# Weight tiles of four feed-forward matrices begun at other byte offsets

## The chip, the cores and the metric

The kernel runs on one NeuronCore of one Trainium2 chip. The time is device microseconds from launch to end; before the change it is 2638.81 us, the median of three runs (2638.7 to 2639.36).

## The reference

Three stages follow each other on 24,576 rows of 128 numbers in float32 (two batches of 12,288):

```
kv_pool = kv averaged over 4x4 patches          # 2 x 768 keys x 128
k = v   = kv_pool @ w_sr
a       = softmax(q @ k.T / sqrt(128))          # rows x 768
x       = a @ v
h = x @ w_in1 ; x = (h * clip(h + 3, 0, 6) / 6) @ w_out1   # 128 -> 2048 -> 128
h = x @ w_in2 ; out = (h * cos(h)) @ w_out2                # 128 -> 2048 -> 128
```

## The kernel before

The rows go through in 48 blocks of 512, with features on the partitions and the block's 512 rows along the free dimension. A number that TensorE is to multiply precisely is held as a sum of two float32r parts, hi and lo, and one product is made of three matmuls: hi by hi, lo by hi and hi by lo. Each of the four weight matrices (in1, out1, in2, out2) lies in SBUF for the whole program as a hi and a lo array of 16 slices of 128x128; a slice is 512 bytes in each partition.

A unit (`plan_unit`) is one layer, one block and two of the 16 slices. `ff_in` (L845) issues six matmuls of 512 columns (L849, L850, L851 for each slice): the slice of `w_in` is the stationary operand, loaded by a weight load that the profile shows as PEld, and the block's `x` tile is the moving one. ScalarE, VectorE and GpSimd make the gated value and split it into a `hi` and a `lo` tile. `ff_out` (L853) then issues six matmuls (L857, L858, L859) with the slice of `w_out` stationary and `hi` or `lo` moving. With 48 blocks, two layers and eight units there are 768 units, and so 768 x 12 = 9,216 such matmuls, 2,304 on each weight matrix.

Attention adds, for each block, 24 float32r matmuls of 384 columns for the scores (L651; a q tile is stationary, the keys move) and six float32 products for the values (L773; `v_all` is stationary, the transposed softmax tile moves), each of which the trace shows as two records. Three early blocks are transposed by TensorE (L565, L742), the others by DMA.

The order on each engine is worked out before the program is written: `Plan.run` simulates the engines with fixed costs and due times and writes the instructions in that order.

All SBUF tiles come from one pool that lays them one behind another in the order in which they are made: constants, keys, values, the eight weight arrays (L283 to L287), then the `w`, `hi`, `lo` and `x` tiles of 4,096 bytes. In the built program the address of each of these, from `w_sr_sb` to the last `x`, leaves 192 when divided by 512; `ident` alone leaves 128. The weights are written once, in the first part of the program, in 16 pieces of four slices, the hi part by ScalarE (L399), the lo part by GpSimd or VectorE (L407).

Of the kernel before, what the change touches and what calls it, by code (L numbers as in the profile page):

```python
# [11 lines left out]
F32R = mybir.dt.float32r  # L12
# [24 lines left out]
SPARE = 5  # L37

NSCR = 3

BY_PE = 3

# [200 lines left out]
def attention_ffn_ffn_kernel(  # L243
# [13 lines left out]
    _, H, W, _ = kv.shape  # L257
    R = 4
    DFF = w_out1.shape[0]
    P = 128  # L260
# [7 lines left out]
    NP = DFF // (2 * P)  # L268
# [3 lines left out]
    const = ctx.enter_context(tc.tile_pool(name="const", bufs=1))  # L272
# [9 lines left out]
    v_all = const.tile([P, NKC, C], F32, name="v_all")  # L282
    weights = {}  # L283
    for n in ("in1", "out1", "in2", "out2"):
        weights[n] = tuple(
            const.tile([P, 2 * NP, P], F32R, name=f"w_{n}_{part}") for part in ("hi", "lo")
        )  # L287

    def tiles(tag, count, shape, dtype, pool=const):
        return [pool.tile(shape, dtype, name=f"{tag}{i}") for i in range(count)]  # L290
# [12 lines left out]
            "two": free_banks,  # L303
            "scrq": tiles("scrq", NSCR, [NJ * P * 2, C], U16, dram),
            "scro": tiles("scro", NSCR, [C * 2, T], U16, dram),
            "scri": tiles("scri", NSCR, [T], F32, dram),
            "scr": tiles("scr", NSCR, [NKC // 2, NJ * P * 2, 2 * P], U16, dram),
        },
# [739 lines left out]
    for i, (n, src) in enumerate(  # L1048
        (("in1", w_in1), ("out1", w_out1), ("in2", w_in2), ("out2", w_out2))
    ):  # L1050
        for part in range(2 * NP // WK):
            k = 4 * i + part
# [33 lines left out]
```

## Time and profile before

| | |
|---|---|
| median of three runs | 2638.81 us |
| span of the profiled execution, first to last instruction | 2637.8 us |
| time of the three runs beyond that span | 0.9 to 1.6 us |
| TensorE busy, share of the span | 2599.3 us, 99% |
| ScalarE, GpSimd, VectorE busy | 2295.6, 2055.5, 2031.0 us |
| mean granted TensorE clock | 0.998 |

The page lists for each engine the time in which at least one instruction was under way. A TensorE matmul overlaps the next one in its records, so the busy time of a line is no measure of its cost; the distance from one start to the next is.

### The profile page before, as it was taken

The page shows a single profiled execution, that of the slowest core. Times are in us where ns is not written, and L with a number is a line of the kernel's source. Part 1 is how long each engine was busy: PE and PEld are TensorE (multiplying, and loading weights), DVE is VectorE, ACT ScalarE, POOL GpSimd, SP SyncE. Part 2 cuts the span into 40 slices and gives each one's busy share as a digit, 9 for nine tenths or more (in the row PEclk, how much of TensorE's full clock was granted, in tenths as well). Part 3 has the DMA queues.
Part 4 walks back from the last instruction along what each step waited for, and adds up shares of the span by engine and source line. Part 5 has one row for each costly group of instructions (what it writes and reads, how often), then busy time and mean ns, then how long its engine had stood idle before and what let it go on. Part 6 is the DMA issues. An engine that isn't in the chain of part 4 may idle for free. (4 is left out here: it accounts for less than half of the span.)

```text
span 2637.8 us, 32119 instructions
## 1 busy us (share of the span) xinstructions
PE 2599.3 (99%) x11148; PEld 2070.3 (78%) x11148; DVE 2031.0 (77%) x1852; ACT 2295.6 (87%) x2642; POOL 2055.5 (78%) x976
## 2 busy tenths in 40 slices
PE   7899999999999999999999999999999999999998
PEld 5678887888788877777778877887788878887887
DVE  7987777787778778887777777777777777877776
ACT  3799898989898988888889898989898989898887
POOL 1878787878787777687778787878787878787777
PEclk9999999999999999999999999999999999999999
DMA  6323443444333454534333443334333433343320
GB/s 184 97 61 96 100 108 77 96 98 107 80 96 94 111 128 104 130 80 102 88 86 93 102 100 80 99 95 107 79 95 98 108 76 96 95 107 79 76 65 28
DMA packets 520722, 250.78 MB, mean 95 GB/s; under 512 B 392560, under 2 KB 488944, under 8 KB 520560
## 3 DMA queue, kind: packets, MB, share of 16 engines
q1 hardware_dynamic: 520560, 248.74, 39.3%
q8 instruction: 87, 1.43, 0.2%
q14 instruction: 75, 0.61, 0.1%
HBM read 46.20 MB, written 107.58 MB: 58 GB/s over the span
## 5 line engine op out<-in xcount | busy, mean ns | idle before, releaser
L887 POOL TENSOR_TENSOR lo<-w,hi 128x1024 fp32r<-128x1024 f32 x768 | 1830.4, 2409 | 439.8 <-ACT hi L911 358.9
L911 ACT CAST hi<-w 128x1024 fp32r<-128x1024 f32 x768 | 781.2, 1056 | 46.7 <-DVE w L884 32.5
L884 DVE TENSOR_TENSOR w<-w,banks 128x1024 f32<-128x1024 f32 x384 | 464.8, 1219 | 243.2 <-ACT w L881 234.3
L857 PE MATMUL banks<-hi,w_out_hi 128*128 128x512 f32 x1536 | 634.8, 413 | 1.0 <-DVE w_out_lo L407 0.6
L849 PE MATMUL banks<-x,w_in_hi 128*128 128x512 f32 x1536 | 621.5, 405 | 9.7 <-DVE w L867 4.8
L875 DVE SCALAR_TENSOR_TENSOR w<-banks,w 128x1024 f32<-128x1024 f32 x384 | 464.4, 1218 | 216.2 <-ACT w L872 216.0
L859 PE MATMUL banks<-lo,w_out_hi 128*128 128x512 f32 x1536 | 600.5, 391 | 1.5 <-POOL lo L887 1.5
L851 PE MATMUL banks<-x,w_in_hi 128*128 128x512 f32 x1536 | 600.2, 391 | 0.0
L858 PE MATMUL banks<-hi,w_out_lo 128*128 128x512 f32 x1536 | 599.3, 390 | 0.0
L850 PE MATMUL banks<-x,w_in_lo 128*128 128x512 f32 x1536 | 599.1, 390 | 0.0
L872 ACT ACTIVATE w<-banks 128x1024 int32<-128x1024 f32 x384 | 389.5, 1027 | 145.6 <-PE banks L851 145.2
L867 DVE SCALAR_TENSOR_TENSOR w<-w,banks 128x1024 f32<-128x1024 f32 x384 | 459.6, 1215 | 23.5 <-ACT w L864 19.0
L881 ACT ACTIVATE w<-w 128x1024 f32<-128x1024 f32 x384 | 405.3, 1069 | 63.2 <-DVE w L875 62.2
L864 ACT ACTIVATE w<-banks,three 128x1024 f32<-128x1024 f32 x384 | 420.0, 1120 | 24.8 <-PE banks L851 24.5
L849 PEld LDWEIGHTS banks<-x,w_in_hi 128*128 128x128 f32 x1536 | 288.4, 188 | 90.1 <-DVE w L884 12.1
L857 PEld LDWEIGHTS banks<-hi,w_out_hi 128*128 128x128 f32 x1536 | 288.8, 188 | 78.4 <-ACT w L872 9.3
L858 PEld LDWEIGHTS banks<-hi,w_out_lo 128*128 128x128 f32 x1536 | 288.8, 188 | 77.2 <-issue 20.8
L850 PEld LDWEIGHTS banks<-x,w_in_lo 128*128 128x128 f32 x1536 | 288.4, 188 | 67.1 <-issue 11.4
L859 PEld LDWEIGHTS banks<-lo,w_out_hi 128*128 128x128 f32 x1536 | 288.5, 188 | 63.1 <-POOL lo L887 1.9
L851 PEld LDWEIGHTS banks<-x,w_in_hi 128*128 128x128 f32 x1536 | 288.2, 188 | 61.7
L714 DVE COPY w<-w 128x1536 uint16<-128x1536 uint16 x180 | 310.3, 1746 | 8.1 <-issue 5.5
L773 PE MATMUL banks<-w,v_all 128*128 128x512 f32 x576 | 270.4, 592 | 0.0
(70 smaller groups left out, 1806.5 us busy)
## 6 DMA issues: line engine op xcount, KB each, us to landing
scr<-w SPq DMA_DIRECT2D x180, 384.0 KB, 2.5
w<-in_kv_dram SPq DMA_DIRECT2D x48, 256.0 KB, 5.1
w<-in_q_dram SPq DMA_DIRECT2D x48, 256.0 KB, 3.4
w<-scri SPq DMA_DIRECT2D x48, 256.0 KB, 4.3
out_dram<-w SPq DMA_DIRECT2D x48, 256.0 KB, 2.0
scro<-w SPq DMA_DIRECT2D x47, 256.0 KB, 2.2
scrq<-w SPq DMA_DIRECT2D x45, 256.0 KB, 2.3
w<-in_moe_w_in_dram SPq DMA_DIRECT2D x8, 512.0 KB, 6.4
```

Source lines behind the costliest of these rows:

```text
L849: nc.tensor.matmul(t[:, i, :], w_hi[:, k, :], xx[:, 0, :], start=True, stop=False)
L850: nc.tensor.matmul(t[:, i, :], w_lo[:, k, :], xx[:, 0, :], start=False, stop=False)
L851: nc.tensor.matmul(t[:, i, :], w_hi[:, k, :], xx[:, 1, :], start=False, stop=True)
L857: nc.tensor.matmul(t, o_hi[:, k, :], h[:, i, :], start=(k == 0), stop=False)
L858: nc.tensor.matmul(t, o_lo[:, k, :], h[:, i, :], start=False, stop=False)
L859: nc.tensor.matmul(t, o_hi[:, k, :], l[:, i, :], start=False, stop=(k == 2 * NP - 1))
L864: nc.scalar.activation(plan[g], two(ps), AF.Relu, bias=three, scale=1.0)
L867: nc.vector.scalar_tensor_tensor(out=plan[g], in0=plan[g], scalar=6.0, in1=two(ps), op0=ALU.min, op1=ALU.mult)
L875: nc.vector.scalar_tensor_tensor(out=plan[g], in0=two(ps), scalar=0.25, in1=plan[g].bitcast(I32), op0=ALU.add, op1=ALU.subtract,)
L884: nc.vector.tensor_tensor(out=plan[g], in0=plan[g], in1=two(ps), op=ALU.mult)
L887: nc.gpsimd.tensor_tensor(out=plan[lo], in0=plan[g], in1=plan[hi].bitcast(F32), op=ALU.subtract)
L911: prio + HI_AT, {"act": 947}, lambda e: nc.scalar.copy(plan[hi], plan[g]), [a],
```

## The change

Each pair of hi and lo arrays becomes one tile of 16,896 bytes per partition, 512 more than the two arrays held, and the arrays are slices of it that begin 2, 4, 8 or 16 float32 numbers (8, 16, 32 or 64 bytes) behind the tile's start. In the built program the four tiles still begin 192 bytes beyond a multiple of 512, so the weights of in1, out1, in2 and out2 begin 200, 208, 224 and 256 bytes beyond one. The tiles made after them lie 2,048 bytes higher, and so keep their 192; those made before stay where they were. Every engine's instructions stand in the order that they had and wait for the same things.

```diff
@@ -37,6 +37,9 @@
 NSCR = 3
+
+SHIFT_ROOM = 128
+SHIFT = {"in1": 2, "out1": 4, "in2": 8, "out2": 16}
 
 BY_PE = 3
@@ -282,8 +285,12 @@
     for n in ("in1", "out1", "in2", "out2"):
+        held = const.tile([P, 2 * DFF + SHIFT_ROOM], F32R, name=f"w_{n}")
         weights[n] = tuple(
-            const.tile([P, 2 * NP, P], F32R, name=f"w_{n}_{part}") for part in ("hi", "lo")
+            held[:, SHIFT[n] + i * DFF : SHIFT[n] + (i + 1) * DFF].rearrange(
+                "p (k f) -> p k f", f=P
+            )
+            for i in range(2)
         )
```

## Rows read from the trace of the kernel before

**Rows 1.** The page's first part, busy us of each engine, and its granted clock
```profile
span 2637.8 us, 32119 instructions
PE 2599.3 (99%) x11148; PEld 2070.3 (78%) x11148; DVE 2031.0 (77%) x1852; ACT 2295.6 (87%) x2642; POOL 2055.5 (78%) x976
...
PEclk9999999999999999999999999999999999999999
```
**Rows 2.** Costliest groups: TensorE and its weight loads; busy us, mean ns | idle
```profile
L857 PE MATMUL banks<-hi,w_out_hi 128*128 128x512 f32 x1536 | 634.8, 413 | 1.0 <-DVE w_out_lo L407 0.6
L849 PE MATMUL banks<-x,w_in_hi 128*128 128x512 f32 x1536 | 621.5, 405 | 9.7 <-DVE w L867 4.8
L850 PEld LDWEIGHTS banks<-x,w_in_lo 128*128 128x128 f32 x1536 | 288.4, 188 | 67.1 <-issue 11.4
```
**Rows 3.** Timeline of two units: start us, us, engine, line, operation
```profile
427.53 0.39 PE L849 MATMUL banks<-x,w_in_hi 128*128 128x512 f32 x1
427.53 0.19 PEld L850 LDWEIGHTS banks<-x,w_in_lo 128*128 128x128 f32 x1
...
427.75 0.39 PE L850 MATMUL banks<-x,w_in_lo 128*128 128x512 f32 x1
...
448.38 0.39 PE L859 MATMUL banks<-lo,w_out_hi 128*128 128x512 f32 x1
```
**Rows 4.** Two stretches: busy us (instructions) of each engine, clock, DMA share, GB/s
```profile
core 0: us, PE busy (x) PEld busy (x) DVE busy (x) ACT busy (x) POOL busy (x), PEclk, DMA share, GB/s
427.52:448.37 20.85, 20.85 (x93) 17.27 (x92) 16.80 (x17) 20.41 (x23) 15.20 (x7) 1.00 0.67 150
419.21:420.25 1.04, 1.04 (x7) 1.04 (x7) 0.66 (x2) 1.04 (x3) 1.04 (x1) 1.00 0.00 0
```
**Rows 5.** Timeline of TensorE where float32 values and transposes stand
```profile
55.37 1.88 PE L773 MATMUL banks<-w,v_all 128*128 128x512 f32 x4
57.09 1.91 PE L742 MATMUL banks<-ident,w 128*128 128x128 f32 x16
```
**Rows 6.** Costliest groups: a single record of those two lines
```profile
L773 PE MATMUL banks<-w,v_all 128*128 128x512 f32 x576 | 270.4, 592 | 0.0
...
L742 PE MATMUL banks<-ident,w 128*128 128x128 f32 x72 | 9.3, 276 | 1.8 <-ACT w L663 0.9 <-ACT w L331 0.8
```
**Rows 7.** Instructions that write the lo part of in1 and in2
```profile
L407 POOL TENSOR_TENSOR w_in_lo<-w,w_in_hi x4: 1295/1300/1304, 48.8 to 66.5; 128x512 fp32r<-128x512 f32 x4
L407 DVE TENSOR_TENSOR w_in_lo<-banks,w_in_hi x4: 673/678/681, 94.6 to 120.4; 128x512 fp32r<-128x512 f32 x4
```

## The prediction, made before the changed kernel ran

> **What bounds the kernel now.** I read the page's first part, then the costliest groups, then TensorE's timeline. The first part says who is the bound: TensorE is busy 2599.3 of 2637.8 us, so it idles 38.5 us in all, at a granted clock in the top tenth in all 40 slices; ScalarE, next, has 342 us of slack [rows 1]. The groups say what it does: the feed-forward lines, 1,536 records each on six lines, with mean records of 405 to 413 ns (where the first of a run is counted long) [rows 2]. These records overlap, so the cost is the distance between starts. The timeline has an unbroken run of them: from the L849 at 427.53 to the L859 at 448.38, 92 steps [rows 3]; 20.85 us / 92 = 226.6 ns a matmul, at a granted clock of 1.00, the 2.4 GHz level [rows 4]. 9,216 x 226.6 ns = 2088 us, 79% of the span. So whatever the weights' place does to this one distance, the whole program feels; whatever it does elsewhere is small.
>
> Then how the 226.6 ns are made up. A run of six score matmuls of 384 columns takes 1.04 us, 173.3 ns each [rows 4] (the count of seven there includes one that was already running). The two lengths differ by 128 columns and 53.3 ns, 0.416 ns a column, which is one column in each cycle of 2.4 GHz. 512 columns are then 213.2 ns, and **13.4 ns are left over in every float32r matmul**, the same for 384 and 512 columns. This remainder is what the change could work on: the weight load for the next matmul begins at the same 427.53 us as the matmul beside it [rows 3] and takes 188 ns [rows 2], so it reads SBUF while the moving tile is read, and both tiles begin 192 bytes beyond a multiple of 512.
>
> **The change part by part.** *Instructions:* none is added, removed or moved, and no wait is; 0 us.
>
> *The distance between the matmuls.* Each of the four matrices has 2,304 matmuls, so 1 ns in the distance is 2.3 us a matrix and 9.2 us for all. No row of before has float32r weights at another residue, so the price is bounded from both sides. Below: the whole remainder goes, -13.4 ns, 2304 x 13.4 = -31 us a matrix and -123 us in all. Above: the weight load takes twice its 188 ns and stands in the way, 376 instead of 226.6 ns, +149 ns, 344 us a matrix. I take 0, from two rows that are nearer than either end.
>
> First, the same residue without the remainder. The values are float32, and their `v_all` and moving tiles both begin at 192 too. Four records take 1.88 us with 0.592 us for the last one alone [rows 5, 6]: 1.288 / 3 = 429 ns. Sixteen transposes of 128 columns take 1.91 us with 0.276 for the last: 1.634 / 15 = 109 ns [rows 5, 6]. Here the two lengths differ by 384 columns and 320 ns, 0.833 ns a column, two cycles; 512 columns are 427 ns, and 2 ns are left over, not 13.4. A weight load as large from the same residue costs these records next to nothing, so the residue by itself does not make the remainder. (Their moving tile is read at half the pace, which could hide a conflict; so this does not exclude one.) And the transposes have `ident` at 128 against tiles at 192, 64 bytes apart, while the values have no distance at all: both fit one line with a remainder of 2 ns.
>
> Second, the remainder does not jitter. In the 92 steps GpSimd, ScalarE, VectorE and the DMA engines work on SBUF for 15 to 20 of 20.85 us [rows 4], the moving buffers change from unit to unit and the weights go on by 512 bytes a slice; 226.6 is the mean, and the starts two steps apart in the rows fit it to the timeline's 0.01 us [rows 3]. A cost that came of two readers meeting in one part of SBUF ought to depend on who else is there. A fixed step of the float32r path ought to look as it does.
>
> [...]
>
> *Writing the weights.* The pieces are written at the new offsets once, near the start; a lo piece takes 0.68 us on VectorE or 1.30 us on GpSimd [rows 7], and TensorE waits for one of them 0.6 us [rows 2]. I take 0; between nothing and a doubling of the eight shown (4 x 0.68 + 4 x 1.30 = 7.9 us), most of it would lie beside TensorE's work.
>
> *The tiles behind.* They move up by 2,048 bytes and keep their residue; the buffers that alternate within the 92 steps lie 4,096 bytes apart, half tiles 2,048, and the distance stays, so 0.
>
> The sum is 0: 2637.8 us of span, and 1.0 us around it as the median of the runs has it, 2638.8 us.
>
> **The rivals.** *A: the remainder is a conflict, and an offset frees it (faster).* For it: exactly the situation in which one could arise, load and matmul reading at the same time from equal residues, and a remainder independent of the columns, as a price per weight load would be. Against it: the values and the missing jitter, above. One matrix freed gives 2639 - 31 = 2608 us, all four 2639 - 123 = 2516 us if no other engine steps in; at ScalarE's 2296 us of work it would not quite reach that. With four offsets a partial result is as likely as a full one.
>
> *B: a start that is not on a whole unit of SBUF makes the weight load dearer (slower).* The place is in1, the only matrix whose slices begin at an odd multiple of 8 bytes (200). The load takes 188 ns and the next can begin after 226.6, so 38 ns of lengthening are hidden; it decides from there. I price it as one more remainder exposed on each of in1's matmuls, as if the load took 240 ns: 2304 x 13.4 = +31 us, 2670 us; the far end is the doubled load, 2983 us. For it: nothing in this trace was ever read from such an address. [...]
>
> *C: the offsets don't reach what matters.* The addresses are 200, 208, 224 and 256 as described, but if what counts is a coarser or finer part of the address, all four fall on the same side. The time is then the forecast's, and the two can't be told apart by this change alone.
>
> **How the numbers follow.** Forecast (with C) 0.70; A 0.15, of which about 0.06 is one matrix or a little more, the rest larger; B 0.15, of which 0.10 is up to the +31 us. The time is the forecast's, 2638.8 us; its own range is 2634 to 2644. The range to hold 8 in 10 reaches to one matrix freed and one matrix made dearer: 2608 to 2670. 0.2% is 5.3 us, about what a measurement of this kernel can tell from no change; it is crossed by 0.57 ns on every matmul or 2.3 ns on those of one matrix. Faster 0.15, same 0.70, slower 0.15.
>
> **What would show it.** If I am right, a run of feed-forward matmuls after the change still steps by 226.6 ns on all six lines, weight loads still take 188 ns, and TensorE is busy 2599 us. [...] B shows as weight loads over 188 ns and steps over 226.6 on the in lines alone, in half of their units. A change of the time with steps unchanged, from waits or the start, would be none of these, and would make the working wrong where it took 0 for the rest.

## The result: 1.4% slower, and the feed-forward step is longer on all four matrices

The changed kernel takes 2676.71 us (2674.53 to 2676.91, three runs) against 2638.81: ratio 1.0139, 95% interval 1.0121 to 1.0157. The forecast of no change was wrong, and so was the range, which ended at 2670. The profile after is of the 2674.53 us run.

First part of its page, to set beside [rows 1]:

```profile
span 2672.6 us, 32119 instructions
PE 2637.8 (99%) x11148; PEld 2074.0 (78%) x11148; DVE 2031.5 (76%) x1852; ACT 2302.1 (86%) x2642; POOL 2058.2 (77%) x976
...
PEclk9999999999999999999999999999999999999999
```

The counts are the same, the clock is the same, VectorE, ScalarE and GpSimd work as long as before within 7 us; TensorE alone is busy 38.5 us longer, and its idle time falls from 38.5 to 34.8 us. No wait was added. The weight loads did not grow either: 188 ns before, 188 or 189 now. Two groups of matmuls and one of weight loads, to set beside [rows 2] (line numbers are 7 higher than before):

```profile
L864 PE MATMUL banks<-hi,w_out 128*128 128x512 f32 x1536 | 644.2, 419 | 1.0 <-DVE w_out L414 0.6
L856 PE MATMUL banks<-x,w_in 128*128 128x512 f32 x1536 | 627.6, 409 | 7.8 <-DVE w L874 4.5
...
L857 PEld LDWEIGHTS banks<-x,w_in 128*128 128x128 f32 x1536 | 288.5, 188 | 71.7 <-issue 11.5
```

What grew is the distance between starts. The first window below holds the 92 steps that [rows 3, 4] hold of before, the next four are unbroken runs on one matrix: 23 steps on in1, 23 on out1, 17 on in2, 37 on out2. Each window counts one matmul more than it has steps, and its bounds are rounded to 0.01 us.

```profile
core 0: us, PE busy (x) PEld busy (x) DVE busy (x) ACT busy (x) POOL busy (x), PEclk, DMA share, GB/s
429.82:451.21 21.39, 21.39 (x93) 17.30 (x92) 17.11 (x17) 20.95 (x24) 15.51 (x7) 1.00 0.65 142
1226.06:1231.38 5.32, 5.32 (x24) 4.24 (x23) 3.02 (x3) 4.53 (x5) 4.69 (x3) 1.00 0.17 49
128.88:134.23 5.35, 5.35 (x24) 4.34 (x23) 5.32 (x7) 5.32 (x8) 0.86 (x1) 1.00 0.45 103
2635.91:2639.87 3.96, 3.96 (x18) 3.19 (x17) 1.23 (x1) 1.99 (x3) 3.96 (x3) 1.00 0.01 4
2655.49:2664.12 8.63, 8.63 (x38) 6.96 (x37) 4.33 (x5) 5.41 (x6) 8.63 (x5) 1.00 0.01 3
```

The 92 steps take 21.39 us instead of 20.85, 232.5 ns each. On one matrix the step is 231 ns for in1 (8 bytes), 233 for out1, in2 and out2 (16, 32, 64 bytes). The last two windows are in the program's tail, where DMA hardly works and VectorE works 1.23 of 3.96 us in the first of them; GpSimd works throughout there, but only 0.86 of 5.35 us in the window on out1. The longer step is in all three, so none of these is needed for it.

Over the whole trace, the mean distance of starts within one matrix (about 1,900 steps each, waits left out) goes from 227.7 to 230.5 ns for in1, 227.5 to 233.4 for out1, 228.2 to 232.9 for in2 and 228.1 to 233.6 for out2. 2,304 x (2.8 + 5.9 + 4.7 + 5.5) = 44 us; some 9 us come back elsewhere, most of them where TensorE had waited or restarted after a value run, and 35 us are left, which is what the span grew by (2672.6 - 2637.8).

### The profile page after: what moved, and what is told of

It reads as the page before. It is cut to its first block, busy times and chain, and to the rows that moved or that the text cites. A ratio compares the mean times of both kernels' runs of the same rounds, so it can differ in the third digit from the quotient of the medians.

```text
span 2672.6 us, 32119 instructions
## 1 busy us (share of the span) xinstructions
PE 2637.8 (99%) x11148; PEld 2074.0 (78%) x11148; DVE 2031.5 (76%) x1852; ACT 2302.1 (86%) x2642; POOL 2058.2 (77%) x976
## 3 DMA queue, kind: packets, MB, share of 16 engines
q1 hardware_dynamic: 520560, 248.74, 38.5%
## 5 line engine op out<-in xcount | busy, mean ns | idle before, releaser
L864 PE MATMUL banks<-hi,w_out 128*128 128x512 f32 x1536 | 644.2, 419 | 1.0 <-DVE w_out L414 0.6
L856 PE MATMUL banks<-x,w_in 128*128 128x512 f32 x1536 | 627.6, 409 | 7.8 <-DVE w L874 4.5
L866 PE MATMUL banks<-lo,w_out 128*128 128x512 f32 x1536 | 607.1, 395 | 1.0 <-POOL lo L894 1.0
L865 PE MATMUL banks<-hi,w_out 128*128 128x512 f32 x1536 | 607.6, 396 | 0.0
L857 PE MATMUL banks<-x,w_in 128*128 128x512 f32 x1536 | 605.0, 394 | 0.0
L858 PE MATMUL banks<-x,w_in 128*128 128x512 f32 x1536 | 604.6, 394 | 0.0
L856 PEld LDWEIGHTS banks<-x,w_in 128*128 128x128 f32 x1536 | 288.7, 188 | 90.3 <-issue 10.5
L864 PEld LDWEIGHTS banks<-hi,w_out 128*128 128x128 f32 x1536 | 289.3, 188 | 84.2 <-issue 11.2
L865 PEld LDWEIGHTS banks<-hi,w_out 128*128 128x128 f32 x1536 | 288.8, 188 | 82.7 <-issue 20.8
L866 PEld LDWEIGHTS banks<-lo,w_out 128*128 128x128 f32 x1536 | 290.4, 189 | 72.0 <-POOL lo L894 1.5
L857 PEld LDWEIGHTS banks<-x,w_in 128*128 128x128 f32 x1536 | 288.5, 188 | 71.7 <-issue 11.5
L858 PEld LDWEIGHTS banks<-x,w_in 128*128 128x128 f32 x1536 | 288.6, 188 | 67.7
```

The source lines that it names most:

```text
L856: nc.tensor.matmul(t[:, i, :], w_hi[:, k, :], xx[:, 0, :], start=True, stop=False)
L857: nc.tensor.matmul(t[:, i, :], w_lo[:, k, :], xx[:, 0, :], start=False, stop=False)
L858: nc.tensor.matmul(t[:, i, :], w_hi[:, k, :], xx[:, 1, :], start=False, stop=True)
L864: nc.tensor.matmul(t, o_hi[:, k, :], h[:, i, :], start=(k == 0), stop=False)
L865: nc.tensor.matmul(t, o_lo[:, k, :], h[:, i, :], start=False, stop=False)
L866: nc.tensor.matmul(t, o_hi[:, k, :], l[:, i, :], start=False, stop=(k == 2 * NP - 1))
```

## The experiments

A tile's residue is what its start address leaves when divided by 512. The distance is the residue of the stationary tile less that of the moving one, and a step is settled when it has stopped changing from one matmul to the next or goes round in a fixed cycle. Theory R: the distance sets the step. Rivals: A, the weights' own address; T, the joined tiles or the moved-up buffers; mixing four shifts. "Steps" below are those 92 steps of the same place in the program, unless another place is named.

**Room without shift.**

```diff
-SHIFT = {"in1": 2, "out1": 4, "in2": 8, "out2": 16}
+SHIFT = {"in1": 0, "out1": 0, "in2": 0, "out2": 0}
```

> All four shifts are 0: the four tiles with room are kept, as is the place of every tile behind them, and weights and moving tiles share their residue again. Theory R (the distance between the residues of weights and moving tiles sets the step between matmuls): steps settle at 226.6 ns as before, 2639 us. Theory A (the address of the weights by itself): the same, 2639 us. Theory T (the joined tiles, or the 2,048 bytes by which the other tiles moved up): 2677 us, steps of 230 to 234 ns.

2638.3 us, ratio to before 1.0000 (0.9991 to 1.0010). The window of 92 steps:

```profile
428.08:448.92 20.84, 20.84 (x93) 17.26 (x92) 16.81 (x17) 20.41 (x23) 15.26 (x7) 1.00 0.66 150
```

The step is 226.5 ns again. T falls; the shift alone is the cause.

**One shift of 64 bytes for all.**

```diff
+SHIFT = {"in1": 16, "out1": 16, "in2": 16, "out2": 16}
```

> All four weight matrices begin 64 bytes beyond the residue of the moving tiles, at 256. After the change out2, alone at this shift, stepped by 233.6 ns on the mean against 228.0 before. Theories R and A: all four matrices step by about 233.6 ns, 5.7 ns more than the 227.9 of before, 9,216 x 5.7 = 53 us, 2691 us. If the mixture of four shifts was what cost (each change of matrix upsets the rhythm), one shift for all is nearer to 2639 us.

2680.49 us, ratio 1.0160 (1.0145 to 1.0175).

```profile
431.01:452.47 21.46, 21.46 (x93) 17.20 (x92) 17.05 (x17) 20.94 (x24) 15.41 (x7) 1.00 0.64 141
```

233.3 ns a step, and steady: 233, 233, 234 over and over. So mixing is not the cause; one distance, held, costs 6.7 ns. The total grew by 42 us, not by the 53 expected. Over the whole trace the mean step grew by 5.3 ns and not 5.7: in the kernel before it had been 227.9, since steps behind the scores are uneven there (below), and those gained less. The rest came back where TensorE had waited or restarted.

**Everything moved by 64 bytes, distance 0.**

```diff
+SHIFT = {"in1": 0, "out1": 0, "in2": 0, "out2": 0}
...
+    const.tile([P, 16], F32, name="pad")
     w_sr_sb = const.tile([P, C], F32, name="w_sr_sb")
```

> 64 unused bytes lie ahead of w_sr_sb, so keys, values, weights and all moving tiles begin 256 bytes beyond a multiple of 512, and weights and moving tiles share their residue; shifts are 0. Theory R: steps settle at 226.6 ns, 2639 us. Theory A: the weights lie at 256 as in the run with all at 64 bytes, so the time is that run's, about 2691 us.

2637.24 us, ratio 0.9994 (0.9985 to 1.0004).

```profile
425.48:446.33 20.85, 20.85 (x93) 17.27 (x92) 16.83 (x17) 20.42 (x23) 15.26 (x7) 1.00 0.66 150
```

The weights lie at the same addresses here as in the run before this one, all at residue 256, and the moving tiles 64 bytes further than there; the step is 226.6 against 233.3 ns. Rival A falls: the address by itself does nothing, the distance to the moving tile does it.

**Two sweeps of four shifts each.**

```diff
+SHIFT = {"in1": 32, "out1": 64, "in2": 96, "out2": 126}   # first sweep
+SHIFT = {"in1": 24, "out1": 40, "in2": 48, "out2": 56}    # second sweep
```

> Shifts of 128 bytes (in1), 256 (out1), 384 (in2) and 504 (out2), the last 8 bytes short of a whole 512. Theory R with a period of 512 bytes and a price that grows with the distance either way: out2 steps like in1 did at 8 bytes, about 230.5 ns, the other three at 233 to 235, sum near 2680 us. Rival R2 (only some distances collide): one of the four steps at 226.6 or less. Rival R3 (any distance but 0 costs the same): all four at 233.5, 2690 us.

> Shifts of 96 bytes (in1), 160 (out1), 192 (in2) and 224 (out2). Theory R: no distance beats 0; mean steps of all four between 229 and 234 ns, sum 2665 to 2690 us. Rival R2 (some distance lets load and moving read pass without meeting): one of the four below 226.6 ns.

2672.71 and 2676.73 us (ratios 1.0130 and 1.0143). Mean distances of starts within one matrix, by shift in bytes, those of the changed kernel included. Each shift stood on one matrix while the other three had others:

```
  8    16    32    64    96   128   160   192   224   256   384   504
230.5 233.4 232.9 233.6 233.7 232.4 233.5 230.2 233.6 229.6 232.3 233.2 ns
```

None is below the 227.5 to 228.2 of before, so none of these distances frees the matmul. The price does not grow with the distance: 8 bytes beyond is cheap, 8 bytes short (504) is not, though I had expected the two to agree. 128 and 384 do agree, a hint at a period of 256.

**All at 256 bytes.**

```diff
+SHIFT = {"in1": 64, "out1": 64, "in2": 64, "out2": 64}
```

> All four shifts are 256 bytes. With out1 at 256 among other shifts, its steps came to 227, 226, 227 within some units, though not in all (229.6 on the mean). Theory R256 (what counts repeats every 256 bytes): steps settle at 226.6 ns everywhere, 2639 us. Rival R512 (the distance has to be 0 modulo 512): steps of 229 to 233 ns, 2655 to 2690 us.

2638.80 us, ratio 1.0000 (0.9991 to 1.0010).

```profile
427.20:448.05 20.85, 20.85 (x93) 17.27 (x92) 16.83 (x17) 20.42 (x23) 15.24 (x7) 1.00 0.65 150
```

226.6 ns: 256 bytes count as 0. With 128 and 384 bytes alike above (232.4 and 232.3 ns), I take the distance modulo 256 bytes as what counts. Among other shifts the same 256 had a mean of 229.6, so a matmul also pays for what its neighbours did. Where they all have that distance it does not: in the first sweep, an unbroken run of 23 steps on out1, the matrix at 256, takes 5.21 us, 226.5 ns each:

```profile
129.11:134.32 5.21, 5.21 (x24) 4.32 (x23) 5.17 (x7) 5.18 (x7) 0.87 (x1) 1.00 0.26 67
```

The price of 8 bytes is not one of its neighbours': the changed kernel's 23 steps on in1 alone had 231 ns.

**All at 192 bytes.**

```diff
+SHIFT = {"in1": 48, "out1": 48, "in2": 48, "out2": 48}
```

> All four weight matrices begin 192 bytes beyond the moving tiles' residue, that is 64 bytes short of it modulo 256: the distance that the q tile has to the keys where scores became faster. Theory D with its sign (64 short is cheap, 64 beyond is dear): feed-forward steps settle at 226.6 ns, 2636 to 2641 us. Rival R (512-column steps are at their best at equal residues): 229 to 231 ns as in2 had at this shift among other shifts (230.2), 2650 to 2670 us.

2649.77 us, ratio 1.0041 (1.0026 to 1.0056), so rival R here, at the edge of its 2650 to 2670 us; its steps go 226, 229, 232 in turn, 228.8 ns:

```profile
427.60:448.65 21.05, 21.05 (x93) 17.28 (x92) 17.00 (x18) 20.61 (x23) 15.42 (x7) 1.00 0.65 148
```

By the period of 256, 192 beyond is 64 short. 64 bytes short of the moving tile cost a third of 64 bytes beyond it: the sign matters.

**Keys moved, weights left.** Four runs on the kernel before move the keys (and in the first the values) against the q tiles; scores are float32r, values float32. A second pad keeps the weights where they were.

```diff
+    const.tile([P, 16], F32, name="pad")       # 32, 48 for 128 and 192 bytes
     k_hi = const.tile([P, KEYS], F32R, name="k_hi")
     k_lo = const.tile([P, KEYS], F32R, name="k_lo")
+    const.tile([P, 112], F32, name="pad2")     # 96, 80; behind v_all in the first run
```

> Built on the kernel before: keys and values alone move up by 64 bytes, to 256; weights and moving tiles share 192. So the scores (float32r, q tile stationary at 192, keys moving at 256) get a distance of 64 bytes, and the values (float32, v_all stationary at 256, moving at 192) too. Theory R as a rule for float32r: score steps go from 173.3 ns when undisturbed (176.9 on the mean) to about 180, 1,152 x 3 to 7 ns = 4 to 8 us; values stay at 428.5 ns a record, since their moving tile is read at half pace; feed-forward steps stay; 2642 to 2646 us. Rival R-all (any matmul pays): 576 value records get 6.7 ns each as well, another 4 us. Rival W (it is something about the weight tiles only): 2638.5 us.

> Built on the kernel before: the keys alone begin 64 bytes further, at 256; v_all is at 192 again. The run with keys and values at 256 took 6 us less than before (score steps 174.1 ns on the mean instead of 176.9). Theory K (the gain is the score matmuls', q tile 64 bytes short of the keys): 2633 us and 174 ns again. Rival V (v_all's place made it): 2638.5 us and 176.9 ns.

> Built on the kernel before: the keys alone begin 128 bytes further, at 320, half of the 256 bytes after which the feed-forward steps repeated. Theory D (each distance has its own price, which half a period makes worst): score steps of 178 to 182 ns, 1,152 x 3 = 2 to 6 us more, 2640 to 2645 us. Rival H (the scores' price is only that of getting into rhythm again after 512-column matmuls, and any distance changes that by chance): 174 to 179 ns, 2634 to 2642 us, with runs of 173.3 ns in some blocks.

> Built on the kernel before: the keys alone begin 192 bytes further, at 384, so the q tile is 64 bytes ahead of the keys modulo 256, which is the distance that out2 had after the change. Theory D: the sign decides; score steps of about 180 ns as feed-forward steps rose by 6.7 ns at this distance, 2642 us. Rival H: 174 to 179 ns, 2634 to 2642 us.

Keys and values at 64: 2632.95 us, ratio 0.9977 (0.9968 to 0.9987). Keys alone: 2633.23, 0.9980 (0.9970 to 0.9989). Keys at 128: 2635.04, 0.9985 (0.9975 to 0.9995). Keys at 192: 2634.13, 0.9981 (0.9971 to 0.9992). My expectation for the first had the wrong sign: a distance other than 0 makes these kernels faster, by 4 to 6 us. The address alone does not: with everything moved by 64 bytes (above) the keys lay at 256 as well, q tiles too, and the ratio was 0.9994. V falls: v_all's place is no part of it. And where v_all lies 64 bytes off its moving tile, a value record keeps its 592 ns and the distance of starts goes from 428.5 to 428.8 ns on the mean; of the first of these runs, against [rows 6]:

```profile
L775 PE MATMUL banks<-w,v_all 128*128 128x512 f32 x576 | 270.5, 592 | 0.0
```

Where the 6 us come from is seen where scores are followed by feed-forward work. Windows of six scores and of the nine feed-forward steps behind them, at one place of the program; the kernel before:

```profile
733.09:734.15 1.06, 1.06 (x7) 1.06 (x6) 0.00 (x0) 1.06 (x2) 1.06 (x2) 1.00 0.02 4
734.16:736.23 2.07, 2.07 (x10) 1.68 (x9) 1.88 (x2) 2.05 (x4) 2.07 (x1) 1.00 0.58 120
```

Keys alone at 64 bytes:

```profile
729.15:730.19 1.04, 1.04 (x7) 1.04 (x6) 0.00 (x0) 1.04 (x2) 1.04 (x2) 1.00 0.00 0
730.20:732.25 2.05, 2.05 (x10) 1.68 (x10) 1.86 (x2) 2.03 (x4) 2.05 (x1) 1.00 0.61 132
```

Keys at 192 bytes:

```profile
729.53:730.59 1.06, 1.06 (x7) 1.06 (x6) 0.00 (x0) 1.06 (x2) 1.06 (x2) 1.00 0.01 2
730.60:732.63 2.03, 2.03 (x10) 1.68 (x10) 1.84 (x2) 2.01 (x4) 2.03 (x1) 1.00 0.63 130
```

In the kernel before the six scores go 170, 175, 178, 185, 176, 181 ns and the nine steps behind them 230, 233, 236, 224, 231, 236, 228, 232, 231, then 226.6 again: after a change of length the steps are uneven and settle only after nine. Keys at 64 shorten the scores (173 ns on the mean) and the way back; at 192 the scores stay at 176 to 178 and the feed-forward steps begin at 227, 226, 227 at once. This is no matter of one place. Each trace has 83 runs of scores with at least 14 feed-forward steps behind them and no wait in these: the steps settle after nine in all 83 in the kernel before, after three or seven in all with the keys alone at 64, after two or three in all at 128, and at once in 78 at 192. In the kernel before the nine steps cost 41 ns over settled ones, by my estimate some 5 us over the 132 places where feed-forward steps follow scores, and the run at 192 gained 4.5. Theory D (a fixed price for each distance) fails here, since 192 was to cost; rival H (the price is that of getting into rhythm again) fits. Of all kernels run, the one with keys and values moved is the fastest, 6 us under the kernel before; with the keys alone the time is the same within the noise.

**Half loads.** Only 64 of 128 weight columns are loaded and used, first by the lo matmuls (L850, L858) alone, then by all six, at distance 0 and at 64 bytes. What the other 64 columns give is left out. One line of the edit:

```diff
-nc.tensor.matmul(t[:, i, :], w_lo[:, k, :], xx[:, 0, :], start=False, stop=False)
+nc.tensor.matmul(t[0:64, i, :], w_lo[:, k, 0:64], xx[:, 0, :], start=False, stop=False)
```

> Built on the kernel before. The matmuls by the lo weights (L850, L858) load and use only the first 64 of 128 columns, so half of their product is left out; the moving side and all distances stay. Theory S (the 13.4 ns that each float32r matmul pays over its columns are paid for the reading of the next weights, at equal residues too): the step during which the half load is read (from L849 to L850, from L857 to L858) falls by about 6.7 ns to 220 ns; 3,072 such steps, 2639 - 20 = 2619 us. Theory F (a fixed cost of each float32r matmul): all steps stay at 226.6 ns, 2639 us.

> Built on the kernel before, equal residues. All feed-forward matmuls load and use only 64 of 128 weight columns, so half of the output features are left out; all loads are alike again, the moving side is whole. Theory S (the 13.4 ns beyond 512 columns are paid for the reading of the load): steps settle at 213.2 + 6.7 = 220 ns, 9,216 x 6.7 = 62 us less, 2577 us. Theory F (a fixed cost of a float32r matmul): steps settle at 226.6 ns, 2639 us.

> The same halved loads, with all four weight matrices 64 bytes beyond the moving tiles' residue. With whole loads this distance added 6.7 ns to the settled step (233.3 against 226.6). If that addition is paid for the reading of the load, half of it stays: 3.3 ns over the step of the halved run at equal residues (223.3 by S, 230 by F; some 31 us over that run). If it is a fixed price of the distance: 6.7 ns (226.7 by S, 233.3 by F; some 60 us over it). If the load is then too short to meet the moving read at this distance: nothing.

2655.24 us (1.0061, 1.0041 to 1.0081), 2655.28 (1.0064, 1.0041 to 1.0087) and 2676.23 (1.0143, 1.0099 to 1.0187). Neither S nor F had this: less to load is slower. (The matmul uses half of its columns too, so the edit does not tell a shorter load from a narrower matmul.) The loads did become shorter, in the first of the three:

```profile
L858 PEld LDWEIGHTS banks<-hi,w_out_lo 128*64 128x64 f32 x1536 | 206.4, 134 | 80.3 <-issue 20.8
```

The 92 steps with the lo loads halved, 229.7 ns a step:

```profile
428.88:450.01 21.13, 21.13 (x93) 15.61 (x92) 17.08 (x18) 20.69 (x23) 15.46 (x7) 1.00 0.67 147
```

With all halved at distance 0, 229.9 ns, in a cycle of 230, 236, 229, 224, 227, 234:

```profile
428.21:449.36 21.15, 21.15 (x93) 12.34 (x92) 17.09 (x18) 20.71 (x23) 15.46 (x7) 1.00 0.66 147
```

With all halved at 64 bytes, 232.5 ns:

```profile
433.17:454.56 21.39, 21.39 (x93) 12.44 (x92) 17.05 (x17) 20.92 (x24) 15.47 (x7) 1.00 0.64 142
```

The extra for 64 bytes falls from 6.7 to 2.6 ns, about as a price in proportion to the load would (3.3 was expected of that), but with half loads at distance 0 the even step of 226.6 ns is gone. Whether its 13.4 ns are paid for the load stays open.

## Why the prediction was wrong

*What bounds the kernel* was right: the one distance between feed-forward matmuls carries the program, and nothing else added time. The 2.4 GHz and the cycles named there are no reading of a clock: they are the 0.416 ns a column worked out from [rows 4], turned round; the trace gives the granted clock only as a share, 1.00. *No cost elsewhere* was right too: the joined tiles and the moved-up buffers cost nothing, as the run with room and no shift shows; a lo piece of the weights at the new offsets is still written in 0.68 or 1.30 to 1.32 us, and TensorE still waits 0.6 us for one.

*The distance between the matmuls*, where I took 0 between -13.4 and +149 ns, is the step that failed. It measured +2.8, +5.9, +4.7 and +5.5 ns a matrix. Both arguments that I leaned on said less than I made of them.
- The values have a remainder of 2 ns at equal residues, and so say nothing for float32r, where equal residues leave 13.4. Values and transposes "fit one line" because two lengths always do. That float32 records hardly feel a distance of 64 bytes was shown only by moving `v_all` (428.5 to 428.8 ns). I had noted that they read their moving tile at half pace (0.833 against 0.416 ns a column) and could hide a conflict, and then let them decide for float32r all the same.
- The lack of jitter spoke of the other engines' accesses, and the 92 steps do go 226 and 227 ns beside them (the rows that I gave for it, 427.53 and 427.75, are one step apart, not two). It said nothing of TensorE's own two reads. A steady step does not exclude a price: at 64 bytes the step is dearer and as steady, 233, 233, 234. The trace held a sign that the remainder is not fixed: the nine uneven steps of 224 to 236 ns after a run of scores, at a granted clock of 1.00. I worked out the mean of an even run and did not ask why others were uneven. The scores' 173.3 ns were an even run too; their mean in the kernel before is 176.2.

*Rival A* had the condition right (the residues of weights and moving tile) and the direction wrong: equal residues are the best case, and none of the distances tried was better for 512 columns. *Rival B*, with 2670 us, came near the time by luck. It expected in1, at 8 bytes, to pay 13.4 ns alone through a longer load; the loads stayed at 188 ns and in1 paid least of the four. So a start at an odd multiple of 8 bytes does not explain the price here: in1, the one matrix that has it (200), pays 2.8 ns, and the other three (208, 224, 256) pay 4.7 to 5.9, about twice as much. *Rival C* is excluded: all four offsets reach what matters.

For float32r it matters where the two tiles lie: 226.6 against 233.3 ns with the weights at the same addresses, depending on whether the moving tiles begin 64 bytes off or not. By what the time is lost, no run shows.

Shown: the float32r step of 512 columns depends on where stationary and moving tile begin against each other (226.6 ns at 0, 233.3 at 64 bytes), with 256 bytes counting as 0 (226.6), on the sign of that distance (228.8 at 64 short) and on the steps before (224 to 236 in the nine after scores). Not shown: what inside TensorE or SBUF makes it so. That load and moving read meet in some part of SBUF and one waits is an argument that fits, not a finding; the half loads contradict its simplest form.

## What to carry to other kernels

Where float32r matmuls bound a kernel, look at the address of stationary and moving tiles modulo 256 bytes: odd-sized small tiles between them can put them apart, and 64 bytes cost 1.6% here (2680.49 us) without any instruction changing. Compare the distance of starts, not the records' durations, and treat uneven steps at full clock as a question about operand placement. Tune it by running, a run of equal matmuls and the change from one length to another apart, for the best distance was 0 for the first and not 0 for the second.

## What the runs showed of the hardware that was not expected

- Settled steps of 512-column float32r matmuls at a granted clock of 1.00: 226.6 ns at distances of 0 and 256 bytes, 233.3 at 64, 228.8 at 192.
- A weight load of 64 columns takes 134 ns, one of 128 takes 188: 0.84 ns a column, an estimate from these two lengths, half the pace of the moving read (0.416 ns, from the steps of 384 and 512 columns). A load of half the size, for a matmul that uses half the columns, made the step longer, 229.9 instead of 226.6 ns.
- After a change from 384 to 512 columns the float32r stream of these runs needs up to nine steps to settle, and the distance of the scores' operands decides how many: nine with the keys at the q tiles' residue, three or seven at 64 bytes, two or three at 128, almost always none at 192.
